# Moving one half of a down projection a step earlier, and re-dealing the opening of a fused gated-linear-attention and SoLU kernel

## The chip, the cores and the metric

The kernel runs on one core of one Trainium2 chip. The metric is the device time of one execution in microseconds; the time given for a kernel is the median of its runs. A profile shows one execution, counted from its first instruction to its last: that length is the span.

## The reference

Two blocks follow each other. The first is a recurrent gated linear attention over 4 batches, 8 heads, 768 positions and 48 features a head; the second is a feed-forward block with the SoLU activation and a layer norm over its 1024 hidden features. q, k, v and alpha come as float32, the weights of the second block as float64.

```python
def _attn_ref(q, k, v, alpha):                 # each (4, 8, 768, 48)
    state = np.zeros((B, H, D, D))
    for t in range(S):
        state = alpha[:, :, t, :, None] * state + np.einsum('bhd,bhe->bhde', k[:, :, t], v[:, :, t])
        y[:, :, t] = np.einsum('bhd,bhde->bhe', q[:, :, t], state)

# bridge: (B, H, S, D) -> x of (B*S, H*D) = (3072, 384)

def _moe_ref(x, w_in, w_out, g_ln):            # w_in (384, 1024), w_out (1024, 384)
    h = x @ w_in
    sm = softmax(h)
    solu = h * sm
    ln = (solu - mean(solu)) / np.sqrt(var(solu) + 1e-06) * g_ln
    return ln @ w_out                          # (3072, 384)
```

## The kernel before

**Groups and batches.** The 768 positions are cut into G = 6 groups of 128. A group holds 128 positions of all B = 4 batches, so 512 tokens. The attention of a group needs the state left by the group before it; its feed-forward part needs only its own attention output. Output block n = 4g + b is batch b of group g.

**The stages of one group.** *Attention:* `alpha_T`, `scan_back`, `inverses` and `scan_on` (VectorE, L204 and L213) make the running products of alpha; keys and queries are multiplied by them (`kT`, `qv`, `qe`); `move_lasts` and `move_firsts` (SyncE, L232 and L237) copy the queries by twelve transfers into `lot`, seen as `q64`, the layout in which they meet the state; `scores` (TensorE L278), `masked` (VectorE L289), `decay` (GpSimd L261, which scales `state` by columns that lie in `lot` too), `read_state` and `read_values` (TensorE L333) give the output, which ScalarE copies into `x` (L363); `next_state` (L371, L381) adds the group's keys and values. *Up:* for each of FC = 8 slices f of the hidden features, `up_mm` (L394, three matmuls, six records in the trace) and `up_act`: e = exp(h) on ScalarE (L408), u = h * e on VectorE (L409), u2 = u * u on ScalarE (L412). The tile h has two buffers, so slice f + 2 can start only when u of slice f is done. *Sums:* `running` adds e on GpSimd and u2 on VectorE over f into `p` (L427), `token_sums` (L462 to L473) turns them into a sum for each token; in the last group VectorE also adds up u itself (L424), and `last_norm` (L485 to L499) uses that. *Down:* `down(n, half)` is four matmuls of one 128-token block against four slices of `w_out` (L507, eight records). *Finish:* `finish(n)` does three small VectorE operations (L532 to L537), the reciprocal root `r` on GpSimd (L546), the scaled output on ScalarE (L548) and a store by SyncE.

**Order.** The order of instructions on every engine is the order in which the source writes them; nothing rearranges it, and each engine takes its instructions in turn. After an opening written out by hand, one loop runs over periods g = 1 to 5 of eight steps s each. In step s it does `up(g, s)`, pieces of the attention of group g + 1 at the places "head", "behind", "middle" and "tail" that two small tables name, and one entry of the list `todo`, which holds the eight halves of the downs of the group before. Period 1 has an empty list, since the downs of group 0 stand in the opening. After a second half, `finish` follows in the next step, ahead of `running`. What remains after period 5 are the eight halves of group 5, with `token_sums` and `last_norm` after the first of them.

**The opening.** While group 0 runs its eight up steps, the float64 weights are turned into float32. They come in eight pieces of 768 columns (`fetch`, SyncE L578, into slots of the tile `room`); `bits` makes float32 of a piece by five VectorE operations (L612, L615, L620, L623, L624) and `in_range` checks its magnitude by two ScalarE operations (L598, L601). Pieces 0 to 3 are `w_in`, 4 to 7 `w_out`, and `scaled` (ScalarE L631) multiplies `w_out` by the layer norm's gain. The first three groups of the five operations of a piece stand after the first, the rest after the second of two up steps: piece 2 + f // 2 in steps f = 0 to 7, and pieces 6 and 7 after the loop. Then come, in the order of the source: the turned keys and queries of group 1 (`turned`, L164), the downs of group 0, `mean(0)` (L645: column sums of `w_out`, copied and scaled by ScalarE, L650), `mean(1)` (L652, copied by ScalarE to `mean_sb`, L653), the copies `hold` of two finished blocks (L516), and the attention of group 1. The checks `alpha_over` (L196) and `fend` (L212) run beside it.

Of the kernel before, what the change touches and what calls it, by code (L numbers as in the profile page):

```python
# [11 lines left out]
U32 = mybir.dt.uint32  # L12
I32 = mybir.dt.int32
AF = mybir.ActivationFunctionType
ALU = mybir.AluOpType
# [17 lines left out]
def fast_path(ctx, tc, q, k, v, alpha, moe_w_in, moe_w_out, moe_g_ln, out):  # L33
# [13 lines left out]
    B, H, S, D = q.shape  # L47
    NTOK, DM = out.shape
    DFF = moe_w_in.shape[1]
    G = S // P  # L50
# [5 lines left out]
    FC = DFF // P  # L56
# [43 lines left out]
    qn = const.tile([P, H, TQ, D], FP, name="qn")  # L100
# [30 lines left out]
    def load(src, dst, g):  # L131
        t = slice(g * P, (g + 1) * P)
        for b in range(B):
            nc.sync.dma_start(
                out=dst[32 * b : 32 * b + 32].rearrange("t h u d -> t h (u d)"),
                in_=src[b, :, t, :].rearrange("h (t u) d -> t h (u d)", u=TQ),
            )
# [49 lines left out]
    def alpha_T(g):  # L187
        nc.gpsimd.memset(aT[:, :, 0:1], 0.0)
        firsts(an, aT[:, 0:H, 1:SW])
        lasts(an, aT[:, H:NB, 1:SW])  # L190
# [43 lines left out]
    def move_firsts():  # L234
        for b in range(B):
            i, c = divmod(b, 2)
            nc.sync.dma_start(out=q64[64 * i : 64 * i + E0, c], in_=qv[32 * b : 32 * b + 32, 0:H])  # L237
# [162 lines left out]
    def up_act(g, f, between=None):  # L400
        d = gr[g]
        h = d["h"]
        if g:
            e, u2 = (ring.tile([P, T4], FP, name=x) for x in ("e", "u2"))
        else:
            e, u2 = (sT[:, f % 4, 4 * i : 4 * i + 4].rearrange("p b t -> p (b t)") for i in range(2))
        u = u_of(g, f)
        nc.scalar.activation(out=e, in_=h, func=AF.Exp)  # L408
        nc.vector.tensor_tensor(out=u, in0=h, in1=e, op=ALU.mult)  # L409
        if between:  # L410
            between()
        nc.scalar.activation(out=u2, in_=u, func=AF.Square)  # L412
        d[f] = e, u2
# [87 lines left out]
    def down(n, half, part=range(HF)):  # L501
        g, b = divmod(n, B)
        d = st[n]
        if half == 0 and 0 in part:
            d["o"] = ps_o.tile([P, 512], FP, tag="o", name="o")
        for f in (half * HF + i for i in part):
            nc.tensor.matmul(  # L507
                d["o"][:, 0 : DM + 1], lhsT=u_of(g, f)[:, b * P : b * P + P], rhs=w_out[:, f], start=(f == 0),
                stop=(f == FC - 1), skip_group_check=True,
            )  # L510

    def hold(n):

        a = 2 * H * SW + (DM + 1) * (n % 2)
        st[n]["held"] = lot[:, a : a + DM + 1]
        nc.scalar.copy(out=st[n]["held"], in_=st[n]["o"][:, 0 : DM + 1])  # L516
# [39 lines left out]
    float64 = moe_w_in.dtype != FP  # L556
# [4 lines left out]
    def place(i):  # L561
        kind, f = pieces[i]
        return w_out[:, f : f + 2, 0:DM] if kind else w_in[:, :, f * P : f * P + 2 * P]
# [22 lines left out]
    made = {}  # L586
# [3 lines left out]
    def in_range(i, parts=(0, 1)):  # L590


        if not float64:
            return
        if 0 in parts:
            hi = raws[i][:, :, :, 1].bitcast(FP)
            squares[i] = one.tile([P, F], FP, name="sq").rearrange("p (c f) -> p c f", c=hi.shape[1])
            nc.scalar.activation(out=squares[i], in_=hi, func=AF.Square, accum_out=far[:, i, 0:1])  # L598
        if 1 in parts:
            sq = squares.pop(i)  # L600
            nc.scalar.activation(out=sq, in_=sq, func=AF.Exp, scale=-(2.0**24), accum_out=far[:, i, 1:2])  # L601

    def bits(i, part=None):
        if not float64:
            return
        lo, hi = raws[i][:, :, :, 0], raws[i][:, :, :, 1]
        if part != 1:
            made[i] = [
                lots[2 * (i % 2) + x].rearrange("p (c f) -> p c f", c=hi.shape[1]) for x in range(2)
            ]  # L610
            top = made[i][0].bitcast(U32)
            nc.vector.tensor_scalar(  # L612
                out=top, in0=hi, scalar1=3, scalar2=0x3FFFFFF8, op0=ALU.logical_shift_left, op1=ALU.bitwise_and
            )
            nc.vector.scalar_tensor_tensor(  # L615
                out=top, in0=hi, scalar=0xC0000000, in1=top, op0=ALU.bitwise_and, op1=ALU.bitwise_or
            )
        if part != 0:
            top, low = made.pop(i)
            nc.vector.tensor_scalar(  # L620
                out=low.bitcast(U32), in0=top.bitcast(U32), scalar1=0xFF800000, scalar2=None, op0=ALU.bitwise_and
            )
            nc.vector.scalar_tensor_tensor(out=low, in0=lo, scalar=2.0**-52, in1=low, op0=ALU.mult, op1=ALU.mult)  # L623
            nc.vector.tensor_tensor(out=place(i), in0=low, in1=top, op=ALU.add)  # L624

    def scaled(i):
# [11 lines left out]
    def mean(half):  # L638


        m = ps_h.tile([P, 512], FP, tag="h", name="sums")[:, 0:DM]
        if half == 0:
            for f in range(FC):
                r = quarter(f % 4)
                nc.tensor.matmul(  # L645
                    m[r], lhsT=ones[:, 0:32], rhs=w_out[:, f, 0:DM], start=f < 4, stop=f >= FC - 4,
                    tile_position=(0, r.start), skip_group_check=True,
                )
            made["m"] = work.tile([P, DM], FP, name="o_mean")
            nc.scalar.mul(out=made["m"], in_=m, mul=-1.0 / (32 * DFF))  # L650
        else:
            nc.tensor.matmul(m, lhsT=ones, rhs=made["m"], start=True, stop=True)  # L652
            nc.scalar.copy(out=mean_sb, in_=m)  # L653
# [50 lines left out]
    for i in range(3):  # L704
        part = slice(NP * i, NP * i + NP)
# [5 lines left out]
    for i in (0, 2, 1):  # L711
        if i == 1:
            scan_on(0, i)
        part = slice(NP * i, NP * i + NP)
        nc.vector.tensor_tensor(
            out=qe[:, :, 0:P] if i == 2 else qv[:, part, 0:P], in0=t[i], in1=aT[:, part, 1:SW], op=ALU.mult
# [13 lines left out]
    keys_back(0)  # L730
    in_range(0)
    bits(1)
    in_range(1)

    for f in range(FC):
        up_mm(0, f)
        if f == 4:
            array_sums(0, 0)
        up_act(0, f, (lambda: in_range(2 + f // 2, (f % 2,))) if f < 6 else None)

        bits(2 + f // 2, f % 2)
        if f == 0:
            next_state(0)
            fetch(4, 3)
            load_first(k, kn, 1)
            load_first(q, qn, 1)
            load(alpha, an, 1)
        elif f == 2:
            ends_k = ends_of(kn, "e")
        elif f == 3:  # L750
            fetch(5, 1)
            fetch(6, 2)
            ends_q = ends_of(qn, "u2")
        elif f == 5:
            fetch(7, 3)
            load_v(1)
        elif f == 6:
            scaled(4)
    bits(6)
    tk = three("tp_k", [(ps_a, "a2"), (ps_a, "a3"), (ps_h, "h")])  # L760
    turned(kn, ends_k, tk)
    load(k, kn, 2)
# [8 lines left out]
    scaled(7)  # L771
    tq = three("tp_q", [(ps_a, "a0"), (ps_a, "a1")])
    turned(qn, ends_q, tq, range(H))
    in_range(5)
    in_range(6)
    for i in range(3):
        scan_back(1, i)
        part = slice(NP * i, NP * i + NP)
        nc.vector.tensor_tensor(out=kT[:, part], in0=tk[i], in1=hk[:, part], op=ALU.mult)
    inverses(1)  # L780
    mean(0)
    down(0, 1)
    mean(1)
    hold(0)
    alpha_over(1)
    load(alpha, an, 2)
    tq += three("tp_q2", [(ps_h, "h")])
    turned(qn, ends_q, tq, range(H, NB))
    load(q, qn, 2)
    down(1, 1)  # L790
    hold(1)
    keys_back(1, three("tp", [(ps_a, "a2"), (ps_a, "a3"), (ps_h, "h")]))
# [2 lines left out]
    apart()  # L795
    ends_of_decay()
    move_lasts()
    in_range(7)
    for i in range(2):
        scan_on(1, i)  # L800
        part = slice(NP * i, NP * i + NP)
        nc.vector.tensor_tensor(out=qv[:, part, 0:P], in0=tq[i], in1=aT[:, part, 1:SW], op=ALU.mult)  # L802
    move_firsts()
    down(2, 0)
    scores(1, 0)
    decay(1)
    masked(0)
    alpha_T(2)
    down(2, 1)
    scores(1, 1)  # L810
    masked(1)
# [98 lines left out]
    for g in range(1, G + 1):  # L910
        rise, att = g < G, g + 1 < G
        plan = first if g == 1 else usual

        def at(where, s):
            for what in plan[where].get(s, "").split() if att else ():
                attend(g + 1, what)

        after = 3 if g == 1 else None
        if not rise:
            break  # L920
        for s in range(FC):
            at("head", s)
            if rise:
                up(g, s)
            if after is not None:
                finish(after)
                after = None
            if s == 0 and g < 3:
                next_state(g)
            if s == 0 and g > 1:  # L930
                token_sums(g - 1)
            at("behind", s)
            for f in centres.get(s, ()) if g == 1 else ():
                centre(f)
            if rise and s:
                running(g, s)
            at("middle", s)
            if todo:
                n, half = todo.pop(0)
                down(n, half)  # L940
                if half:
                    after = n
            at("tail", s)
        if after is not None:
            finish(after)
        todo = [(n, half) for n in range(g * B, g * B + B) for half in range(2)]


    for n, half in todo[:2]:
# [490 lines left out]
```

## Time and profile before

| | |
|---|---|
| three runs | 374.28, 375.96, 377.16 us; median 375.96 us |
| profiled execution | 377.03 us, span 375.2 us |
| TensorE matmuls busy | 362.3 us, 97% of the span |
| VectorE, ScalarE, GpSimd busy | 246.8, 147.0, 125.4 us |
| mean granted TensorE clock | 0.995 |
| TensorE busy from 144.0 to 345.5 us | 201.5 of 201.5 us |
| TensorE busy from 66.5 to 104.05 us | 33.90 of 37.55 us, mean clock 0.95 |

The profiled execution lies 1.83 us above its span, which is what the start and the end of the program take outside it. A line of the chain of waits names who waited, for whom, and then the total in us, the number of waits and the longest. A line of the timeline gives the start, the length, the engine, the source line, the operation, the tiles, the count of instructions merged, and in brackets the idle time just before and what ended it. TensorE records overlap by about 0.15 us, since the next matmul enters before the last one has left; the distance from one start to the next is the cost of a matmul in a stream.

### The profile page before, as it was taken

The numbers are of one execution on the slowest core, as the hardware profiler recorded it, in microseconds if no ns is written. First come the engines' busy times: TensorE is split into PE (matmuls) and PEld (weight loads), VectorE is DVE, ScalarE is ACT, GpSimd is POOL, SyncE is SP. The second block draws the span as 40 slices with busy tenths as digits, with TensorE's granted clock in tenths as the row PEclk, the third lists the DMA queues.
The fourth block names the chain that finished last, engine by engine and source line by source line (L and its number), as shares of the span: only waits on it lengthen the run. The fifth ranks groups of instructions, "written<-read, shape, count | busy, mean of one in ns | idle before, by whom it ended". The sixth has DMA issues, their size and how long they took to land. (4 is left out here: it accounts for less than half of the span.)

```text
span 375.2 us, 10040 instructions
## 1 busy us (share of the span) xinstructions
PE 362.3 (97%) x4341; PEld 216.4 (58%) x4341; DVE 246.8 (66%) x375; ACT 147.0 (39%) x260; POOL 125.4 (33%) x129
## 2 busy tenths in 40 slices
PE   8989999898999999999999999999999999999994
PEld 8775355464755565556575556575555565555652
DVE  1997979979988978954756954756955224544500
ACT  3649853870366253351532251532241231332100
POOL 7020000002347892664112664113673211333200
PEclk9999999999899999999999999999999999999999
DMA  9996986076158706554035354005041000000011
GB/s 179 180 328 158 202 275 134 0 159 124 66 119 178 166 17 132 124 127 113 23 87 106 84 134 107 24 3 107 14 108 35 24 23 0 24 22 21 24 45 49
DMA packets 72871, 36.06 MB, mean 96 GB/s; under 512 B 48232, under 2 KB 70000, under 8 KB 72816
## 3 DMA queue, kind: packets, MB, share of 16 engines
q1 hardware_dynamic: 71792, 34.39, 38.8%
q10 hardware_dynamic: 1024, 0.92, 0.7%
q8 instruction: 36, 0.59, 0.7%
q14 instruction: 19, 0.16, 0.1%
HBM read 25.30 MB, written 4.72 MB: 80 GB/s over the span
## 5 line engine op out<-in xcount | busy, mean ns | idle before, releaser
L507 PE MATMUL o<-w_out,room 128*128 128x385 f32 x384 | 134.9, 496 | 0.0
L394 PE MATMUL h<-x,w_in 128*128 128x512 f32 x288 | 132.2, 599 | 0.6 <-ACT x L363 0.6
L507 PEld LDWEIGHTS o<-w_out,room 128*128 128x128 f32 x384 | 71.6, 191 | 55.0 <-issue 14.4
L394 PEld LDWEIGHTS h<-x,w_in 128*128 128x128 f32 x288 | 52.9, 190 | 58.2 <-issue 48.8
L409 DVE TENSOR_TENSOR room<-h,e 128x512 f32<-128x512 f32 x40 | 27.6, 690 | 61.3 <-ACT e L408 61.2
L408 ACT ACTIVATE e<-h 128x512 f32<-128x512 f32 x40 | 23.8, 596 | 95.8 <-PE h L394 95.5
L427 POOL TENSOR_TENSOR p<-p,e 128x512 f32<-128x512 f32 x30 | 42.9, 1429 | 26.9 <-ACT e L408 26.6
L412 ACT ACTIVATE u<-room 128x512 f32<-128x512 f32 x40 | 25.2, 630 | 36.1 <-DVE room L409 36.1
L546 POOL TENSOR_TENSOR r<-sums,mhalf 128x1 f32<-128x1 f32 x20 | 12.5, 626 | 73.8 <-DVE sums L537 73.8
L289 DVE TENSOR_TENSOR sT<-a,mask 128x512 f32<-128x512 f32 x43 | 26.7, 682 | 13.2 <-PE a L278 13.2
L427 DVE TENSOR_TENSOR p<-p,u 128x512 f32<-128x512 f32 x30 | 24.9, 829 | 7.2 <-ACT u L412 7.2
L204 DVE TENSOR_TENSOR_SCAN hT<-aT,unit 128x516 f32<-128x516 f32 x18 | 23.6, 1356 | 7.6 <-ACT aT L697 7.6
L204 DVE TENSOR_TENSOR_SCAN aT<-aT,seed 128x516 f32<-128x516 f32 x18 | 27.8, 1576 | 0.2
L278 PEld LDWEIGHTS a<-qv,kT 32*128 32x128 f32 x704 | 21.2, 187 | 7.1 <-POOL r L546 1.6
L278 PE MATMUL a<-qv,kT 32*128 32x128 f32 x704 | 23.8, 278 | 0.5 <-DVE qv L802 0.5
L212 POOL COPY fend<-hT 128x12 f32<-128x12 f32 x6 | 4.0, 668 | 59.5 <-DVE hT L204 59.5
L333 PE MATMUL y<-sT,vn 128*32 128x128 f32 x768 | 22.8, 274 | 1.1 <-issue 0.8
L333 PEld LDWEIGHTS y<-sT,vn 128*32 128x32 f32 x768 | 20.7, 110 | 4.4 <-issue 3.8
L225 POOL TENSOR_TENSOR kT<-kT,hT 128x1024 f32<-128x1024 f32 (+1 forms) x8 | 14.2, 1793 | 20.1 <-DVE kT L179 17.8
L196 ACT ACTIVATE sq<-an,mone 128x1536 uint8<-128x1536 f32 x12 | 18.9, 1575 | 0.2
L548 ACT ACTIVATE o_sb<-o,r 128x384 f32<-128x384 f32 x16 | 9.3, 580 | 24.1 <-POOL r L546 24.1
L333 PEld LDWEIGHTS y<-lot,state 64*32 64x32 f32 x640 | 9.5, 108 | 9.6 <-issue 5.8
(148 smaller groups left out, 370.5 us busy)
## 6 DMA issues: line engine op xcount, KB each, us to landing
vn<-in_v_dram SPq DMA_DIRECT2D x24, 192.0 KB, 4.5
an<-in_alpha_dram SPq DMA_DIRECT2D x20, 192.0 KB, 4.2
out_dram<-o_sb SPq DMA_DIRECT2D x20, 192.0 KB, 2.0
room<-in_moe_w_out_dram SPq DMA_DIRECT2D x8, 384.0 KB, 4.6
kn<-in_k_dram SPq DMA_DIRECT2D x16, 192.0 KB, 4.6
qn<-in_q_dram SPq DMA_DIRECT2D x16, 192.0 KB, 4.2
lot<-qe SPq DMA_DIRECT2D x40, 64.5 KB, 2.1
lot<-qv SPq DMA_DIRECT2D x20, 129.0 KB, 2.4
```

What stands on the lines that cost most here:

```text
L196: nc.scalar.activation(out=sq, in_=x, func=AF.Relu, scale=sign, bias=mone, accum_out=over[:, g, i : i + 1])
L204: nc.vector.tensor_tensor_scan(out=o, data0=a, data1=s, initial=1.0, op0=ALU.mult, op1=ALU.add)
L225: nc.gpsimd.tensor_tensor(out=kT[:, part], in0=kT[:, part], in1=hk[:, part], op=ALU.mult)
L278: nc.tensor.matmul(a[b][:, i], lhsT=kT[quarter(b), kb], rhs=qv[quarter(b), qb, 0:P], start=not last and not i, stop=bool(last), tile_posit ...
L289: nc.vector.tensor_tensor(out=sT[:, b, half * NP : half * NP + NP], in0=a[b], in1=mask[:, None, :].to_broadcast([P, NP, P]), op=ALU.mult,)
L333: nc.tensor.matmul(y_bank(b)[quarter(r), a], lhsT=lhsT, rhs=rhs, start=(b, r) not in begun, stop=stop, tile_position=(row, 32 * r), skip_g ...
L394: nc.tensor.matmul(h, lhsT=w_in[:, a, f * P : (f + 1) * P], rhs=d["x"][:, a].rearrange("p b t -> p (b t)"), start=(a == 0), stop=(a == KC ...
L408: nc.scalar.activation(out=e, in_=h, func=AF.Exp)
L409: nc.vector.tensor_tensor(out=u, in0=h, in1=e, op=ALU.mult)
L412: nc.scalar.activation(out=u2, in_=u, func=AF.Square)
L427: eng.tensor_tensor(out=p, in0=d[0][i] if f == 1 else p, in1=d[f][i], op=ALU.add)
L507: nc.tensor.matmul(d["o"][:, 0 : DM + 1], lhsT=u_of(g, f)[:, b * P : b * P + P], rhs=w_out[:, f], start=(f == 0), stop=(f == FC - 1), skip ...
```

## The change

The diff has these parts.

1. **Halves of downs.** In periods 1 to 4, step 7 appends the first half of block 4g, the first of the period's own group, to `todo` and so runs it there; the list for the next period begins with the second half. Period 1 gets one down that it did not have, periods 2 to 4 run the same number as before, each one step sooner, and period 5 has none in step 7. `finish` moves with them, from steps 2, 4, 6 and the end of a period to steps 1, 3, 5 and 7.
2. **Conversions.** The five operations of pieces 2 to 7 are one list, dealt out as 4, 2, 2, 2, 5, 2, 3 and 10 to the eight steps of group 0, thirty in all. `bits(6)` behind the loop goes; `bits(7)` behind it stays, ahead of `token_sums(0)`, so the five operations of piece 7 stand in the program twice: 35 of these operations follow the start of the loop where there were 30.
3. **Checks.** `in_range(1)` moves from ahead of the loop into step 4; piece 4's check moves into step 5 whole, those of pieces 2 and 3 stay; those of pieces 5, 6 and 7 move from ahead of `mean(0)` and from behind `move_lasts` to a place behind `alpha_T(2)`.
4. **Around the mean.** `down(0, 1)` is split: two matmuls ahead of `mean(1)`, two behind it.
5. **A load.** `load(q, qn, 2)` moves on SyncE's queue from ahead of the twelve transfers of `move_lasts` and `move_firsts` to behind them.

The five operations of `bits` are the same as before, each under its own number.

```diff
@@ after the attention of group 0
     bits(1)
-    in_range(1)
+    steps = [(i, step) for i in range(2, 8) for step in range(5)]
+    checks = {0: [(2, 0)], 1: [(2, 1)], 2: [(3, 0)], 3: [(3, 1)], 4: [(1, 0), (1, 1)], 5: [(4, 0), (4, 1)]}
+
+    def check(f):
+        for i, part in checks.get(f, ()):
+            in_range(i, (part,))
 
     for f in range(FC):
         up_mm(0, f)
         if f == 4:
             array_sums(0, 0)
-        up_act(0, f, (lambda: in_range(2 + f // 2, (f % 2,))) if f < 6 else None)
-
-        bits(2 + f // 2, f % 2)
+        up_act(0, f, lambda: check(f))
+        for _ in range((4, 2, 2, 2, 5, 2, 3, 10)[f]):
+            step = steps.pop(0)
+            if float64:
+                bit(*step)
...
-    bits(6)
     tk = three("tp_k", [(ps_a, "a2"), (ps_a, "a3"), (ps_h, "h")])
     turned(kn, ends_k, tk)
...
     scaled(6)
     bits(7)
     token_sums(0)
     alpha_T(1)
...
     turned(qn, ends_q, tq, range(H))
-    in_range(5)
-    in_range(6)
...
     mean(0)
-    down(0, 1)
+    down(0, 1, (0, 1))
     mean(1)
+    down(0, 1, (2, 3))
     hold(0)
...
     turned(qn, ends_q, tq, range(H, NB))
-    load(q, qn, 2)
...
     move_lasts()
-    in_range(7)
...
     move_firsts()
+    load(q, qn, 2)
     down(2, 0)
     scores(1, 0)
     decay(1)
     masked(0)
     alpha_T(2)
+    for i in range(5, 8):
+        in_range(i)
     down(2, 1)
...
             at("middle", s)
+            if s == FC - 1 and g < G - 1:
+                todo.append((g * B, 0))
             if todo:
                 n, half = todo.pop(0)
                 down(n, half)
...
-        todo = [(n, half) for n in range(g * B, g * B + B) for half in range(2)]
+        todo = [(n, half) for n in range(g * B, g * B + B) for half in range(2)][g < G - 1 :]
```

More of the change, by code (lines that the diff above doesn't have):

```diff
@@ L601, in in_range, with bits, bit @@
             nc.scalar.activation(out=sq, in_=sq, func=AF.Exp, scale=-(2.0**24), accum_out=far[:, i, 1:2])
-    def bits(i, part=None):
-        if not float64:
-            return
+    def bits(i, steps=range(5)):
+        for k in steps if float64 else ():
+            bit(i, k)
+    def bit(i, k):
         lo, hi = raws[i][:, :, :, 0], raws[i][:, :, :, 1]
-        if part != 1:
+        if k == 0:
             made[i] = [
@@ L610, in bits @@
             ]
-            top = made[i][0].bitcast(U32)
+        top, low = made[i]
+        bits_top = top.bitcast(U32)
+        if k == 0:
             nc.vector.tensor_scalar(
-                out=top, in0=hi, scalar1=3, scalar2=0x3FFFFFF8, op0=ALU.logical_shift_left, op1=ALU.bitwise_and
+                out=bits_top, in0=hi, scalar1=3, scalar2=0x3FFFFFF8, op0=ALU.logical_shift_left, op1=ALU.bitwise_and
             )
+        elif k == 1:
             nc.vector.scalar_tensor_tensor(
-                out=top, in0=hi, scalar=0xC0000000, in1=top, op0=ALU.bitwise_and, op1=ALU.bitwise_or
+                out=bits_top, in0=hi, scalar=0xC0000000, in1=bits_top, op0=ALU.bitwise_and, op1=ALU.bitwise_or
             )
-        if part != 0:
-            top, low = made.pop(i)
+        elif k == 2:
             nc.vector.tensor_scalar(
-                out=low.bitcast(U32), in0=top.bitcast(U32), scalar1=0xFF800000, scalar2=None, op0=ALU.bitwise_and
+                out=low.bitcast(U32), in0=bits_top, scalar1=0xFF800000, scalar2=None, op0=ALU.bitwise_and
             )
+        elif k == 3:
             nc.vector.scalar_tensor_tensor(out=low, in0=lo, scalar=2.0**-52, in1=low, op0=ALU.mult, op1=ALU.mult)
+        else:
             nc.vector.tensor_tensor(out=place(i), in0=low, in1=top, op=ALU.add)
```

## The prediction

> **What bounds the kernel now.** I read the page first: TensorE is the engine to look at, and its clock drops once.
>
> ```profile
> span 375.2 us, 10040 instructions
> ...
> PE 362.3 (97%) x4341; PEld 216.4 (58%) x4341; DVE 246.8 (66%) x375; ACT 147.0 (39%) x260; POOL 125.4 (33%) x129
> ...
> PEclk9999999999899999999999999999999999999999
> ```
>
> What TensorE does not do is the whole field: 375.2 - 362.3 = 12.9 us, of which the start and the last finish take part. Next, the waits of TensorE alone, to see where it stands still.
>
> ```profile
> PE y L333 <- POOL state L261: 1.7, 1, 1.7
> ...
> PE sums L652 <- ACT o_mean L650: 0.7, 1, 0.7
> ...
> PE h L394 <- ACT x L363: 0.6, 1, 0.6
> PE sums L645 <- DVE cols L467: 0.6, 1, 0.6
> PE tp_q L164 <- ACT mean_sb L653: 0.6, 1, 0.6
> PE a L278 <- DVE qv L802: 0.5, 1, 0.5
> ```
>
> All lie between 66 and 140 us. From 144 to 345.5 us TensorE never rests, so nothing moved there can gain. Then the timeline, to see what stands behind each wait, and the windows around the drop of the clock.
>
> ```profile
> 34.35 0.69 DVE L409 TENSOR_TENSOR room<-h,sT 128x512 f32<-128x512 f32 x1 [1.90 <-ACT sT L408]
> ...
> 61.99 0.55 DVE L612 TENSOR_SCALAR lot<-room 128x768 uint32<-128x768 uint32 x1
> ...
> 66.03 0.44 DVE L467 STREAM_TRANSPOSE cols<-rows 128x256 f32<-128x256 f32 x1
> ...
> 93.06 0.55 PE L333 MATMUL y<-lot,state 64*32 64x128 f32 x16 [1.66 <-POOL state L261]
> ...
> 340.59 0.60 ACT L408 ACTIVATE e<-h 128x512 f32<-128x512 f32 x1 [3.18 <-PE h L394]
> ...
> 343.34 1.35 POOL L427 TENSOR_TENSOR p<-p,e 128x512 f32<-128x512 f32 x1
> ```
>
> ```profile
> 91.51:94.92 3.41, 1.61 (x65) 1.00 0.02 5
> 94.92:98.34 3.42, 3.42 (x36) 0.50 0.32 115
> ```
>
> From 66.03 to 81.71 us VectorE works without a pause, and its last product there (`qv`, L802) releases `scores(1, 0)`: in this stretch VectorE, not TensorE, sets the pace. The window columns are length, TensorE busy, granted clock, DMA share and GB/s: 1.61 us busy in 3.41, then half speed for as long.
>
> **The change, part by part.**
>
> *Conversions and check 1 (VectorE).* Today e of step 0 waits for check 1 on ScalarE, 31.79 to 33.83 us, though h was ready at 31.62. With that check gone it starts at 31.79, u follows 0.61 later at 32.40, and VectorE's idle 1.90 us ends. I walk on with start-to-start distances from the rows: 0.59, 0.98, 0.58, 1.00 and 0.89 for a piece's five operations (4.04), 0.61 for u, 2.64 for an up step on TensorE. u then starts at about 32.45, 36.6, 39.1, 41.95, 44.9, 49.55, 52.0 and 55.1, and the thirty operations end at 63.8 instead of 66.03: 2.2 us sooner (of 3.85 us idle, 1.6 remain, each waiting for e). No up step waits: the nearest, step 7, enters at 50.7 and needs u of step 5, done at 50.2. But `bits(7)` still stands behind the loop, so piece 7 is converted again: 61.99 to 66.03 is the row, 4.04 us. `cols` starts at 63.8 + 4.0 = 67.8, **1.8 us later** than now. Bounds: all idle gone, +0.2; none but step 0's gone, +2.1.
>
> *Around the mean (TensorE).* It is free at 65.96. The column sums wait for `cols` to release their buffer: 66.53 + 1.8 = 68.3, a stall of 2.35 instead of 0.57 us. Behind them the 0.66 and 0.57 us are covered: sums to 69.9 (1.56), half a down to 71.25 (1.38, as at 102.65 to 104.05), by when `o_mean` is ready, since the checks of pieces 5 and 6 (67.18 to 71.09) no longer stand before it; `mean(1)` to 72.1, half a down to 73.45. Its turned queries start there instead of 73.09. The cover of these two stalls is that half down; without it they return, 1.2 us.
>
> *Scores.* TensorE comes to `scores(1, 0)` at 80.80 + 0.36 = 81.2; VectorE releases it at 81.77 + 1.8 = 83.55. Everything up to `read_state(0)` follows in the same distances: 91.40 + 1.8 = 93.2.
>
> *The load and the twelve transfers.* SyncE: `load(alpha, an, 2)` follows `alpha_over(1)`, which follows `hold(0)` at 73.5 (now 72.94), so it issues from 77.3 to 79.15; the q load (78.60 to 80.48) is no longer next, and the first transfer of `qe` goes at 79.85, when `qe` is made (77.98 + 1.8), not 80.59. The fifth and seventh no longer wait for the q load to land (SyncE's waits: 1.1 us). With today's spacing the state is released at 93.06 - 0.74 = 92.3, before TensorE comes at 93.2. So `read_state(0)` starts 0.1 us later than now and does not stop again for 0.25 us: -0.1 in sum. If the transfers should land as late as now (92.03) nothing changes either. The q load, now issued near 90, is first read at 115.24 (L182) and has 25 us of cover, against 7.7 from issue to landing now. The three late checks (2 us each) fall into ScalarE's idle 12.67 us before 94.79; behind them stand only outputs that wait for GpSimd.
>
> *The clock.* The wait of 1.66 us leaves, and with it, I take it, the half-speed window. Its price: the four records from 94.81 take 2.78 us where those from 102.65 take 1.40, and `read_state(1)` 1.43 where 133.85 to 134.94 is 1.09: 1.72 us. Bounds 0 and -1.72; I take -1.72, as no wait is left there. The Trainium skill, "TensorE: Matmul & The Clock Gate", section "Why this matters for your kernels", wants gaps of more than about 3 us before the clock falls to half; this trace has it fall after 1.8 us of rest in 3.41. By the page the drop would not be the wait's, and the sum would be 1.72 us higher.
>
> *Halves of downs.* At the end of period 1 eight records (2.64 us) come between `read_values` and the next up step, which covers the wait for `x` (0.60) and that for `p` at 143.83 (0.24): -0.84. In periods 2 to 4 one down replaces another in TensorE's order, at no cost. The finish moved into step 7 puts three VectorE operations (0.5 us), `r` and `o_sb` ahead of the last sums and the copies of `x`; 2.64 us of down and 1.57 of `next_state` cover that; without them about 1.1 us in each of three periods. The last period loses its cover: `token_sums(5)` follows one half down instead of two, and finish(19) stands before `running(5, 7)`, just as finish(18) does in step 6 now. There e starts at 340.59 and GpSimd's sum ends at 344.69, 4.10 later. From 345.75 that gives 349.85; TensorE arrives at 345.49 + 2.64 = 348.1: a new stall of **+1.75** us. Bounds: 0.8 if `p` ended as now (348.92), 1.9.
>
> *Sum.* -0.1 - 1.72 - 0.84 + 1.75 = -0.9. On the profiled execution, 377.03 - 0.9 = 376.1. The median is 1.07 lower; if its execution had a half-speed window too, it gives 375.05, if it had none, 376.8. I keep **376.1 us**: no change that a measurement could tell (about 1%, 3.8 us).
>
> **The rivals.**
>
> *The second conversion is hidden.* If VectorE loses nearly all its idle time, `cols` starts only 0.2 us later than now and scores is released at 82.0: another 1.6 us gone, 374.5. For it: 3.85 us of idle time lie in the loop. Against: e of each step comes only when TensorE has made h. Had the call behind the loop gone too, the same walk would give `cols` at 63.8, `read_state(0)` at about 89.3 and 372.5 for the profiled execution; that the diff leaves it is what denies the gain.
>
> *Slower: the clock drops after the stall at scores.* Place: 81.2 to 83.55 us, 2.35 us of rest, and the half-speed window falls on scores and the two downs after it. Price: at most 1.72 us, all on the path to `read_state(0)`, so 377.8. It decides when the rest inside one clock window comes to about the 1.80 us seen above, and 1.15 (71.03 to 74.44, where the clock stayed whole) is not enough. For it: the stall is long enough. Against: the stall of 2.35 us before the column sums comes first, and if the clock drops there, TensorE arrives at scores 1.5 us later, which VectorE's lateness hides, and the second stall shrinks to 0.9. The same drop after the last sums would add as much again.
>
> *The dealt conversions starve the up steps.* If the operations on raw words run at the 0.96 us seen at 34.96 instead of 0.55, u of step 5 comes 0.4 to 0.8 us later and step 7 waits; everything after is late by at most 0.5, hidden by the stall before the sums: 376.1 again, or 376.6 at worst.
>
> **How the numbers follow.** Forecast (375 to 377.3 us) 0.55; the hidden conversion 0.16; the slower clock 0.22; starved up steps and the rest 0.07. Faster by over 1%, below 372.2 us, needs 3 us more than the hidden conversion gives beyond the sum's own error: 0.07. Slower by over 1%, above 379.7, needs two or more half-speed windows: 0.12. Within 1%: 0.81. Range: from 374.5 less the median's distance, 373.4, to 376.1 with two windows, 379.4; the likeliest case alone has 375.0 to 377.3.
>
> **What would show it.** Right: 45 conversion operations of all eight pieces instead of 40; `cols` at 67 to 68.5 us; waits of over 2 us before the column sums and of about 2 before scores on `qv`; no wait of `y` for `state`; no wait for `x` at the end of period 1; a wait of `rows` for `p` of 1.3 to 1.9 us near the end. Wrong: `cols` earlier than 66 us, `state` still awaited, or a time below 373 or above 379.5 us.

## The result, and the profile after

The changed kernel takes 376.63 us (20 runs, 375.30 to 378.04), the kernel before 374.95 us (20 runs, 373.93 to 377.16). The medians are 1.7 us apart, the means, 376.42 and 375.14 us, 1.3. The ratio over all runs is 1.0035, 95% interval 1.0022 to 1.0049: 1.3 us slower, within the 1% that the prediction called no change. The median is 0.5 us above its 376.1 us.

The profiled executions say the opposite: 375.56 us with a span of 373.8 after, 377.03 and 375.2 before. The execution profiled before was one of the slowest of its kernel. Why is the main finding below.

The page of the changed kernel:

```profile
span 373.8 us, 10040 instructions
...
PE 361.8 (97%) x4341; PEld 216.4 (58%) x4341; DVE 249.0 (67%) x380; ACT 146.3 (39%) x260; POOL 132.2 (35%) x129
...
PEclk9999999899999999999999999999999999999999
```

VectorE has 380 instructions where it had 375: the five operations of piece 7, done twice. The dip of the clock has moved from the eleventh slice to the eighth. The waits of TensorE in the changed kernel (who waited, for whom: total us, times, longest):

```profile
PE sums L651 <- DVE cols L467: 2.4, 1, 2.4
PE rows L462 <- POOL p L427: 1.7, 1, 1.7
...
PE a L278 <- DVE qv L812: 0.5, 1, 0.5
```

The waits for `state`, `o_mean`, `mean_sb` and `x` are gone; the wait for `cols` has grown from 0.57 to 2.36 us, and one for `p` is new. The timeline of the changed kernel at the places that the prediction named:

```profile
67.77 0.44 DVE L467 STREAM_TRANSPOSE cols<-rows 128x256 f32<-128x256 f32 x1
...
83.41 2.06 PE L278 MATMUL a<-qv,kT 32*128 32x128 f32 x62 [0.50 <-DVE qv L812]
...
92.98 1.17 PE L333 MATMUL y<-lot,state 64*32 64x128 f32 x64
...
345.15 0.60 ACT L408 ACTIVATE e<-h 128x512 f32<-128x512 f32 x1 [3.18 <-PE h L394]
...
347.90 1.35 POOL L427 TENSOR_TENSOR p<-p,e 128x512 f32<-128x512 f32 x1
...
349.30 0.65 PE L462 MATMUL rows<-p,ones 128*32 128x64 f32 x32 [1.66 <-POOL p L427]
```

`cols` starts 1.74 us later than before, scores 1.64 later, and `read_state(0)` 0.08 sooner, without a wait. At the end GpSimd's sum is done 4.10 us after e begins (345.15 to 349.25), and TensorE rests 1.66 us. The windows of the clock in the changed kernel (length, TensorE busy, granted clock, DMA share, GB/s):

```profile
64.81:68.22 3.41, 1.10 (x42) 1.00 0.02 5
68.22:71.63 3.41, 3.36 (x17) 0.50 0.00 0
```

The stall before the column sums leaves TensorE 1.10 us of work in 3.41, and the clock is halved for the next 3.41. That slows the column sums and a half down, but scores waits for VectorE anyway: in this execution the half-speed window costs next to nothing.

### The profile page after: what moved, and what is told of

Same layout as the page of the kernel before. It is cut to its first block, busy times and chain, and to the rows that moved or that the text cites. A ratio compares the mean times of both kernels' runs of the same rounds, so it can differ in the third digit from the quotient of the medians.

```text
span 373.8 us, 10040 instructions
## 1 busy us (share of the span) xinstructions
PE 361.8 (97%) x4341; PEld 216.4 (58%) x4341; DVE 249.0 (67%) x380; ACT 146.3 (39%) x260; POOL 132.2 (35%) x129
## 5 line engine op out<-in xcount | busy, mean ns | idle before, releaser
L427 POOL TENSOR_TENSOR p<-p,e 128x512 f32<-128x512 f32 x30 | 43.7, 1456 | 20.0 <-ACT e L408 19.9
L546 POOL TENSOR_TENSOR r<-sums,mhalf 128x1 f32<-128x1 f32 x20 | 14.8, 741 | 71.2 <-DVE sums L537 71.0
L427 DVE TENSOR_TENSOR p<-p,u 128x512 f32<-128x512 f32 x30 | 22.4, 746 | 5.2 <-ACT u L412 5.2
L212 POOL COPY fend<-hT 128x12 f32<-128x12 f32 x6 | 3.1, 508 | 60.8 <-DVE hT L204 60.8
L261 POOL TENSOR_TENSOR state<-state,lot 128x384 f32<-128x384 f32 x10 | 8.8, 903 | 13.9 <-DMA lot<-qv 13.9
```

Source lines behind the costliest of these rows:

```text
L427: eng.tensor_tensor(out=p, in0=d[0][i] if f == 1 else p, in1=d[f][i], op=ALU.add)
L546: nc.gpsimd.tensor_tensor(out=r, in0=s[:, 3:4], in1=mhalf, op=ALU.pow)
```

## The experiments

The kernel before ran beside each set; its median moved from 374.95 to 375.51 us between sets, so the ratios, which go by all runs and not by the medians, are what is compared. 0.001 is 0.375 us.

The mean clock of a run tells whether a half-speed window fell in it. Of the fourteen profiled executions, leaving out the last ten microseconds of each, the six without such a window have 0.996 to 1.000, the seven with one 0.992 to 0.995, and the one with three 0.985.

| kernel | median, us | ratio to before, 95% interval |
|---|---|---|
| the change | 376.63 | 1.0035, 1.0022 to 1.0049 |
| e1_once | 372.04 | 0.9923, 0.9904 to 0.9942 |
| e2_late | 375.04 | 1.0015, 0.9998 to 1.0031 |
| e3_halves | 375.45 | 1.0016, 1.0001 to 1.0032 |
| e4_sums | 374.99 | 1.0000, 0.9980 to 1.0019 |
| e5_once_sums | 369.63 | 0.9866, 0.9843 to 0.9888 |
| e6_fill_both | 375.55 | 1.0019, 1.0001 to 1.0038 |
| e7_fill_sums | 381.49 | 1.0196, 1.0162 to 1.0229 |
| e8_before_fill | 375.29 | 1.0009, 0.9990 to 1.0027 |
| e9_once_load | 374.11 | 0.9969, 0.9950 to 0.9988 |
| e10_swap | 376.95 | 1.0024, 1.0007 to 1.0041 |
| e11_before_twice | 381.51 | 1.0149, 1.0127 to 1.0172 |
| e12_once_undealt | 375.06 | 0.9980, 0.9959 to 1.0001 |

**What is the second conversion of piece 7 worth?** (e1_once, on the changed kernel)

```diff
     scaled(6)
-    bits(7)
     token_sums(0)
```

> The changed kernel without the second conversion of piece 7 (bits(7) behind the loop is gone, the thirty dealt operations stay). Theory, VectorE's chain sets the pace up to read_state(0): cols starts at 63.7 us instead of 67.8, the stall before the column sums is under 0.1 us instead of 2.36, scores starts near 79.5 instead of 83.4, read_state(0) near 89.4 instead of 93.0, so 3.3 to 3.9 us less than the changed kernel, 372.7 to 373.3 us by its median of 376.63. Rival, the second conversion is hidden behind other waits (the state's release, the clock): within 0.8 us of the changed kernel.

372.04 us: 0.0112 of ratio, 4.2 us below the changed kernel; between the two profiled executions it is 3.1 (375.56 to 372.46). The timeline of e1_once:

```profile
63.72 0.44 DVE L467 STREAM_TRANSPOSE cols<-rows 128x256 f32<-128x256 f32 x1
...
89.03 1.16 PE L333 MATMUL y<-lot,state 64*32 64x128 f32 x64
...
114.08 2.27 PE L278 MATMUL a<-qv,kT 32*128 32x128 f32 x64 [0.29 <-POOL qv L253]
...
124.97 1.02 PE L333 MATMUL y<-lot,state 64*32 64x128 f32 x48 [0.56 <-POOL state L261]
```

`cols` and `read_state(0)` come 4.05 and 3.95 us sooner, so up to there VectorE's chain carries five operations of 4.04 us to TensorE one for one. In the attention of the next group 0.85 us of it is lost again, in two waits that the changed kernel does not have, which leaves the 3.1 of the profiles. The rival, that other waits hide the second conversion, is out. The medians are further apart than the profiles: none of the six runs has a mean clock under 0.996, where seventeen of the changed kernel's twenty have.

**The same from the other side** (e11_before_twice, on the kernel before)

```diff
     bits(7)
+    bits(7)
     token_sums(0)
```

> The kernel before with bits(7) called twice in a row behind its loop, nothing else changed. Theory, VectorE's chain sets the pace and the second call costs its whole 4.04 us: cols at 70.1 us, scores at 85.8, and the copies, the load and the transfers shift with it, so that the state is still awaited: 3.5 to 4.3 us more than the kernel before, 378.5 to 379.4 us by 375.01, or 1 to 1.5 us more where the clock falls. Rival, the wait for the state takes up a part: 1.7 to 2.5 us more.

0.0149, or 5.6 us: above the bare 4.04, inside what was allowed for the clock. `cols` is at 69.95 as expected, but scores at 87.41 instead of 85.8 and `read_state(0)` at 98.36. TensorE's windows in e11_before_twice say why:

```profile
66.00:69.41 3.41, 0.00 (x0) 1.00 0.00 0
69.41:76.23 6.82, 5.78 (x21) 0.50 0.00 0
96.70:100.10 3.40, 1.53 (x59) 1.00 0.14 29
100.13:103.54 3.41, 3.41 (x35) 0.50 0.34 120
```

One whole window without a matmul, then two at half speed, in which the mean comes late for all that follows it, and a third behind the wait for the state. That the chain costs its length is right, that it costs no more was not. The state is still awaited, as expected, though TensorE comes at 97.06 us instead of 91.40: the transfers moved with the chain (the first at 86.24 instead of 80.59). The timeline of e11_before_twice:

```profile
98.36 0.55 PE L333 MATMUL y<-lot,state 64*32 64x128 f32 x16 [1.30 <-POOL state L261]
99.47 1.23 PE L333 MATMUL y<-lot,state 64*32 64x128 f32 x48 [0.56 <-POOL aT L188]
```

**What is the dealing worth?** (e12_once_undealt, on e1_once: the counts, pieces 6 and 7 and checks 1 and 4 as before the change)

```diff
     bits(1)
+    in_range(1)
...
-        for _ in range((4, 2, 2, 2, 5, 2, 3, 10)[f]):
+        for _ in range((2, 3, 2, 3, 2, 3, 2, 3)[f]):
...
+    bits(6)
     tk = three("tp_k", [(ps_a, "a2"), (ps_a, "a3"), (ps_h, "h")])
...
+    bits(7)
     token_sums(0)
```

> The kernel with one conversion of piece 7 (372.04 us) with the conversions dealt as before (2 and 3 a step, pieces 6 and 7 behind the loop) and the checks of pieces 1 and 4 at their old places; all else as in the changed kernel. Theory, dealing and check 1 are worth the 2.2 us by which cols moved: cols back at 65.9 to 66.2 us, scores at 81.7, and 1.9 to 2.3 us slower, 373.9 to 374.4 us. Rival, the gain of that kernel comes from the load and the mean and not from the dealing: within 0.7 us.

0.0057 above e1_once, 2.1 us, as expected; the absolute time is higher because the kernel before was 0.4 us higher in this set too. The agreement is in part luck: eight of the twelve runs have a mean clock of 0.992 to 0.995 and so a half-speed window, which e1_once has in none, and the other four mean 374.21 us, 1.8 us above e1_once once the 0.4 is taken off. The timeline of e12_once_undealt:

```profile
65.97 0.44 DVE L467 STREAM_TRANSPOSE cols<-rows 128x256 f32<-128x256 f32 x1
```

So the dealing and check 1 bring `cols` forward by 2.2 us, and the second conversion takes 4.04.

**What is the moved load worth?** (e9_once_load, on e1_once)

```diff
     turned(qn, ends_q, tq, range(H, NB))
+    load(q, qn, 2)
     down(1, 1)
...
     move_firsts()
-    load(q, qn, 2)
```

> The kernel with one conversion of piece 7 (372.04 us) with load(q, qn, 2) back ahead of the twelve transfers. Theory, once VectorE's chain is short the transfers set read_state(0): their issue starts 1.9 us later and the state is released near 91.5 us, the wait of y for state is 1.9 to 2.6 us instead of 0.6, and the kernel 1.4 to 2.2 us slower, 373.4 to 374.2 us, or up to 1 us more where the clock falls behind that rest. Rival, the transfers are covered: within 0.5 us.

0.0046 above e1_once, 1.7 us, and the wait is back. The timeline of e9_once_load:

```profile
89.89 0.55 PE L333 MATMUL y<-lot,state 64*32 64x128 f32 x16 [1.17 <-POOL state L261]
91.00 1.02 PE L333 MATMUL y<-lot,state 64*32 64x128 f32 x48 [0.56 <-POOL aT L188]
```

The state came sooner than the 91.5 us expected, yet TensorE rests 1.73 us for its two halves, and four of twelve runs have a mean clock of 0.992 to 0.994. What the move is worth in the changed kernel itself was not run. That VectorE is later there does not make it worthless: in e11_before_twice, with a late chain and the load at its old place, the state is awaited all the same. In e9_once_load GpSimd begins to scale the state 2.88 us later than in e1_once (88.99 against 86.11), and TensorE's read starts 0.90 us after that. The changed kernel begins at 90.56 and TensorE comes at 92.98, so by an estimate from these rows the old place would bring a wait of 1.4 us back.

**The halves of downs, taken away and alone** (e2_late on the changed kernel, shown here; e3_halves puts the same lines into the kernel before)

```diff
-            if s == FC - 1 and g < G - 1:
-                todo.append((g * B, 0))
...
-        todo = [(n, half) for n in range(g * B, g * B + B) for half in range(2)][g < G - 1 :]
+        todo = [(n, half) for n in range(g * B, g * B + B) for half in range(2)]
```

> The changed kernel with the halves of the downs as they were before (empty list in period 1, eight entries in periods 2 to 5). Theory, the early halves cost 1.66 us at the last sums and save 0.6 to 0.84 at the end of period 1 and nothing else: 0.8 to 1.1 us less than the changed kernel, 375.5 to 375.8 us, with no wait of rows for p, and a wait for x of about 0.6 us back at the end of period 1. Rival, the finish moved into step 7 costs in the middle periods too: over 1.7 us less.

> The kernel before with the early halves of the downs alone. Theory: the same 0.8 to 1.1 us, now lost against the kernel before: 375.8 to 376.1 us by its median of 374.95; the wait of rows for p is 1.6 to 1.7 us. Rival, the early half gains by itself: the kernel before or less.

Without them the change is at 1.0015, 0.75 us less; alone they cost 0.0016, 0.6 us. Both lie a little under the 0.8 to 1.1 us expected, and the intervals are as wide as the effect. The profiles are clear: e2_late has no wait of `rows` and its wait for `x` is back (0.6 us), e3_halves has the 1.66 us wait of `rows` and none for `x`. A line of the waits of e2_late, then one of the timeline of e3_halves:

```profile
PE h L394 <- ACT x L363: 0.6, 1, 0.6
```

```profile
348.85 0.65 PE L462 MATMUL rows<-p,ones 128*32 128x64 f32 x32 [1.66 <-POOL p L427]
```

So the early half costs a little where it stands: it covers one stall and opens a longer one.

**The cover of the last sums** (e4_sums, on the changed kernel; e5_once_sums, on e1_once)

```diff
     for n, half in todo[:2]:
         down(n, half)
-        if half == 0:
+        if half == 1:
             token_sums(G - 1)
             last_norm()
```

> The changed kernel with token_sums(5) and last_norm behind the second half of block 20 instead of the first. Theory, the wait of rows is the loss of the end and a half down (2.64 us) covers it whole: 1.66 us less than the changed kernel, 375.0 us, with no wait of rows. Rival, the reciprocal root and the finish of block 20 come too late then and TensorE waits for a buffer of o, or the end gets longer: 0 to 0.5 us less.

> Both edits together: the second conversion of piece 7 is gone and token_sums(5) stands behind the second half of block 20. Theory, the two prices are independent: 372.04 - 1.66 = 370.4 us, 1.2% below the kernel before, with no wait of rows and none of over 0.1 us for cols. Rival, the end has another wait behind that of rows: 371 to 372 us.

e4_sums: 0.0035 less, 1.3 us, and no wait of `rows`. e5_once_sums: 0.0057 less than e1_once, 2.1 us, where 1.66 was expected; each of the two ratios is known to about 0.8 us. It takes 369.63 us, 1.34% less than the kernel before (0.9866, interval 0.9843 to 0.9888), the fastest of all. What TensorE still waits for in e5_once_sums, all of it:

```profile
PE warm L452 <- DVE ones L690: 1.1, 1, 1.1
PE a L278 <- DVE qv L811: 0.6, 1, 0.6
PE h L394 <- DVE g_col L642: 0.5, 1, 0.5
PE tp_k L164 <- DMA kn<-in_k_dram: 0.4, 1, 0.4
PE a L278 <- POOL qv L253: 0.3, 1, 0.3
PE y L333 <- DVE sT L289: 0.2, 1, 0.2
PE a L278 <- ACT qv L245: 0.2, 1, 0.2
```

**Is it the rest that halves the clock, and does its place matter?** The idle matmuls of these kernels write to columns of o that nobody reads.

```diff
+    def fill(n, count):
+        t = st[n]["o"][:, DM + 1 : 512]
+        for i in range(count):
+            nc.tensor.matmul(t, lhsT=ones, rhs=ones[:, 0 : 512 - DM - 1], start=False, stop=False, skip_group_check=True)
...
+    fill(1, 10)                 # e6_fill_both and e7_fill_sums
     mean(0)
...
     down(2, 0)
+    fill(2, 9)                  # e6_fill_both
     scores(1, 0)
...
     down(3, 0)
+    fill(3, 7)                  # e8_before_fill, on the kernel before
     read_begin()
```

> The changed kernel with idle matmuls put where TensorE rests: ten of 127 columns ahead of the column sums and nine ahead of scores(1, 0), written to columns of o that nobody reads. Nothing waits for them, and they add 0 to 0.4 us where they outlast the rest. Theory, the rests make the clock fall to half speed in the next 3.41 us, and where that falls behind scores it costs 1.3 us or so: with both filled no run has such a window, the mean clock is 0.997 or more, and the median is that of the lower half of the changed kernel's runs, 375.3 to 375.8 us. Rival, the half-speed window comes without the rests: clock 0.993 to 0.995 as in the changed kernel and 376.6 us or more.

375.55 us, mean clocks of 0.996 to 1.000 in all twelve runs, eleven of them between 375.18 and 375.98 (the last 377.33, at a clock of 1.000, so not by the window). In the two profiles `read_state(0)` starts 64.30 us behind the first up step of group 0 with the fills and 64.30 without: they delay nothing, and there is no half-speed window before the end. The changed kernel's own 20 runs fall into eight at 375.30 to 376.08 and twelve at 376.59 to 378.04; with the fills all runs but one lie in the lower lot. By ratio the gain is 0.0016, 0.6 us, with intervals that overlap; by the medians 1.1.

> The changed kernel with the ten idle matmuls ahead of the column sums alone. Theory, the clock no longer falls there, TensorE comes to scores(1, 0) early, rests over 2 us, and the half-speed window falls behind scores in most runs, on the path: median 376.5 to 377.2 us, the profile has the window after 81 us and no wait of sums for cols over 0.5 us. Rival, where the window falls does not matter, or a rest has nothing to do with it: the median of the kernel with both places filled, within 0.4 us.

381.49 us: neither theory foresaw it. The timeline of TensorE in e7_fill_sums:

```profile
142.97 0.52 PE L462 MATMUL rows<-p,ones 128*32 128x64 f32 x23
146.43 0.48 PE L462 MATMUL rows<-p,ones 128*32 128x64 f32 x9 [2.94 <-issue]
```

Up to 143 us it runs as with both fills (`rows` at 142.97 and 142.91); then TensorE stands 2.94 us in the middle of 32 equal matmuls and waits for nothing that the profile shows, and the clock is halved behind it. So the time says nothing of the question, which e10_swap puts again without added instructions. The profile says something: TensorE rests 0.53 and 1.38 us at `scores(1, 0)`, as the theory has it, but the clock stays whole behind these rests, against it. They are cut by the border between two windows. TensorE's window in e7_fill_sums:

```profile
81.54:84.95 3.41, 2.03 (x61) 1.00 0.53 120
```

> The kernel before with seven idle matmuls ahead of read_state(0), where TensorE rests 1.1 to 1.7 us. Theory, the half-speed window that its first profile shows is in a fifth to a quarter of its runs alone (those of mean clock 0.994 to 0.995, near 376.1 us) and goes with the rest: no run under 0.996, the median 0 to 0.5 us below the kernel before, none over 375.8 us. Rival, the window is in most runs: over 1 us below; or not the rest's: no difference in the clocks.

No run has a mean clock under 0.996, as expected, but the ratio is 0.0009 above the kernel before (interval 0.9990 to 1.0027) and two runs are at 376.1 us. The window goes with the rest; taking it away gains nothing that can be measured, which fits with few of the runs of the kernel before having it.

```diff
     inverses(1)
+    down(0, 1, (0, 1))          # e10_swap, on the changed kernel
     mean(0)
-    down(0, 1, (0, 1))
     mean(1)
```

> The changed kernel with the first half of down(0, 1) ahead of mean(0) instead of behind it; the same instructions in another order. The half down fills 1.38 of the 2.36 us of rest before the column sums, and the time of VectorE's chain does not change. Theory, with 1.0 us of rest the clock no longer falls there; TensorE rests over 1.9 us at scores(1, 0) and the half-speed window falls behind it, on the path, in most runs: median 376.6 to 377.3 us, the profile has the window at 83 to 89 us. Rival, the place of the window does not matter: 375.3 to 376.2 us.

376.95 us, inside the expected. TensorE's windows in e10_swap, and then in e4_sums:

```profile
80.57:83.98 3.41, 1.21 (x16) 1.00 0.53 116
83.99:87.40 3.41, 3.41 (x59) 0.50 0.50 112
```

```profile
81.26:84.67 3.41, 1.49 (x35) 1.00 0.62 127
84.67:88.08 3.41, 3.41 (x41) 0.50 0.46 100
```

With the stall before the sums cut to 0.86 us the clock holds there; the rest at scores grows to 2.2 us and the window falls on the path. Seven runs of e10_swap have a mean clock of 0.993 to 0.995 and mean 377.24 us, five have 0.997 and mean 375.81: 1.4 us is what the window costs there. e4_sums, which has the changed kernel's opening, shows the same window behind scores in its profile, and e2_late, with the same opening too, had it behind the sums; so both happen to one and the same code. What differs is where the borders of the windows fall. In the changed kernel's profile the stall before the sums lies whole in the window from 64.81 to 68.22 us. In e4_sums the same stall of 2.36 us is cut by a border at 67.60, the clock holds, TensorE comes to scores early, and its rests there, 0.54 and 1.38 us, share one window. TensorE's first of these windows in e4_sums:

```profile
64.19:67.60 3.41, 2.00 (x65) 1.00 0.02 5
```

## Why the prediction was right, point by point

- *VectorE's chain.* Right, to 0.1 us: 2.2 us won by dealing (e12_once_undealt 2.1), 4.04 lost to the second conversion (e1_once), `cols` predicted at 67.8 and found at 67.77. The kernel without the second conversion, priced at 372.5 us for the profiled execution, had 372.46 in its own and a median of 372.04. That near a hit is in part luck: 376.1 less the 3.9 us between 93.2 and 89.3 is 372.2, and the two waits of the next group, 0.85 us, were not in the sum.
- *Sums, mean, scores, state.* Right: the stall of 2.36 us (2.35), the two waits behind it gone, scores at 83.41 (83.55), no wait for the state, `read_state(0)` at 92.98 (93.2). One stall took the place of three. GpSimd was done with the state at 92.21 us (92.3), though the first transfer went at 80.50 and not 79.85, behind a load of alpha issued from 78.60 and not 77.3. No run has the changed kernel with the load at its old place, but e11_before_twice makes the moved load, and not the late chain alone, the likely reason that the wait is gone. The half-speed window made TensorE later at scores, as the text on the slower rival had it: it rested 0.50 us there, so the sign "about 2 before scores" did not come in this profile.
- *The clock: the step that was mis-sized.* The -1.72 us is in the two profiled executions, and that is why they show a gain: from `read_state(0)` to the next up step they take 10.99 us before and 8.97 after. It is not in the medians. In 81 runs of the kernel before that ran beside the experiments, 13 have a mean clock of 0.995 or less and mean 376.39 us; the other 68 mean 375.00. So the window is worth 13/81 x 1.4 = 0.2 us on average, and e8_before_fill found nothing. A single execution held a rare event, and the sum took it as the rule. The text kept the other case (376.8 us, a median without a window), and that one was the nearer.
- *The slower rival very likely happened as well.* It was given 0.22 and put at 377.8 us. Seventeen of the 20 runs of the changed kernel have a mean clock of 0.993 to 0.995, five of them at 375.56 to 376.08 us and twelve from 376.59 on. That the twelve are those with the window behind scores is not shown run by run, since one execution alone was profiled; e10_swap and e4_sums show the mechanism and e10_swap its price.
- *Halves of downs.* Right in mechanism: -0.84 and +1.75 were predicted, -0.84 and +1.66 are in the profile, and the runs give +0.6 to +0.75 for the pair. The rule read from step 6 of period 5, that the sum on GpSimd ends 4.10 us after e when a finish stands before it, held to the hundredth.
- *The sum again,* with what the runs showed: -0.1 for the opening, -0.2 for the old window, -0.84 + 1.66 for the halves, and 1.3 us (the distance of the two lots' means, 375.64 and 376.94) in 12 of 20 runs, 0.8: together +1.3 against a measured +1.3. That the forecast's 376.1 us came so near was luck. The sum of -0.9 has the wrong sign and is 2.2 us too low: 1.5 for the window that was credited and 0.8 for the one behind scores that was left out, less 0.1 of the halves. The base, 377.03 us, was 2.1 above the median of many runs, and the two errors all but undid each other. The upper end of the prediction's range, two windows on 376.1, comes to 379.5 and not 379.4.
- *Hidden conversion, starved up steps.* Neither came: `cols` was 1.74 us late, and TensorE has no wait for u in the loop.

## What to carry to other kernels

Count the operations of a re-dealt list against what stays behind it: one call left over turned a change worth 0.8% into one that costs 0.35%, and it shows in the instruction count of the engine (375 to 380) before any run. Where one engine sets the pace of a stretch, a gap closed on another engine only moves to the next meeting point of the two, so follow the slow engine's chain to the end before crediting a wait. Do not credit a clock event that one profiled execution shows until the mean clocks of many runs say how often it comes.

## What the runs showed of the hardware

The clock's windows are 3.41 us long, and what counts in them is the sum of TensorE's work, not the length of one gap. In the fourteen profiles, leaving out the start, before the clock's first record, and the last ten microseconds of a span, every window with 1.61 us of busy time or less was followed by one at half speed (1.61, 1.55, 1.49, 1.49, 1.22, 1.10, 1.06, 0.51 and 0.00), and every one at full clock with 1.75 or more by one at full speed (1.75 in e1_once, e3_halves and e9_once_load). The border lies near half a window: a rest of 1.66 us at the last sums never halved the clock, 1.80 in all before `state` did. Rests of 1.4 and 0.5 us halved it where they shared a window (e4_sums) and did not where a border lay between them (e7_fill_sums, 2.03 us of busy time). In the last ten microseconds the rule fails once: e8_before_fill keeps the full clock behind a window with 1.41 us of busy time. Why is open. TensorE's windows there:

```profile
367.01:370.42 3.41, 1.41 (x5) 1.00 0.05 19
370.42:373.83 3.41, 0.00 (x0) 1.00 0.14 49
```

The Trainium skill, "TensorE: Matmul & The Clock Gate", section "Why this matters for your kernels", names gaps of about 3 us. These traces show the clock fall without one: the longest rest in the window of e4_sums was 1.38 us.

TensorE can also stand still for 2.94 us with no wait to show for it (e7_fill_sums). In that execution a 16 KB packet of the queue that the page calls "instruction" starts at 143.5 us, where the stall begins; e6_fill_both, with nine more matmuls, has no such stall. The changed kernel has a packet of that queue at 143.51 us and does not stand still, so the packet alone is not enough. What the cause is, and why ten added matmuls bring it, was not settled; all six runs of e7_fill_sums take 380.08 us or more.
